# VectorE's order inside the units of a two-branch kernel: three reorderings

## The chip, the cores and the metric

The kernel runs on one core of a Trainium2 chip. The metric is device time in microseconds (us) for one execution. In the profile PE is TensorE, DVE is VectorE, ACT is ScalarE, POOL is GpSimd and SP is SyncE, which here only issues DMAs.

## The reference

The result is `x` plus two branches, in fp32. One is a spectral filter on the layer-normed input, the other a mixture of eight experts of which all eight are chosen, so that the routing only weighs them.

```python
xn = _layernorm(x)                                   # x: (1, 2048, 512)
def _A_ref(x, w_r, w_i):
    X = jnp.fft.rfft2(x, axes=(-2, -1)) * (w_r + 1j * w_i)
    return jnp.fft.irfft2(X, s=(S, D), axes=(-2, -1))
def _B_ref(x, wg, w1, w2):                           # E=8, K=8, D=512, F=1792
    gates = softmax(x @ wg)                          # all 8 kept and normalised
    h = gelu(einsum("nd,edf->nef", x, w1))
    y = einsum("nef,efd->ned", h, w2)
    return einsum("ne,ned->nd", cw, y)
return x + _A_ref(xn, A_w_r, A_w_i) + _B_ref(xn, B_wg, B_w1, B_w2)
```

## The kernel before

**Expert work.** The hidden columns of all experts are cut into 56 chunks of 256. The first two run in a plain stage (`mm1`, `mm2`, with its side work listed in `plan`, L793), which ends at about 138 us. The other 54 run in pairs, each pair on one half of the tokens at a time: 27 pairs by 2 halves are the **units** u = 0 to 53 of the loop at L1301. A product of two 2x2-blocked matrices is done with Strassen's scheme, in Winograd's form: seven block products for the first layer (`layer1`, L991) and seven for the second (`layer2`, L1133), so a unit is 14 products. Each product is 12 matmuls of 128x128 by 128x512, because each fp32 operand is split into a high and a low fp32r part (`high` casts on ACT, `low` subtracts on DVE or POOL) and three of the four partial products are kept. In every product the eight matmuls on the high part of the moving operand come first, and the four on its low part last.

**Steps.** A unit has seven steps n = 0 to 6. `layer1` is a generator with three parts per step; `layer2` of the unit before, called `second`, runs one product a step, woven in between. So TensorE's order in a unit is, with the bank of PSUM each is summed into: a11 (B), b22 (C), a12 (B), T3 (C), s2 (A), b11 (B), s1 (A), b21 (B), s4 (A), T1 (C), s3 (B), T4 (C), a22 (B), T2 (A). Names with a or s first are the first layer's weights, b and T the second layer's hidden blocks. Several products are summed into a bank that still holds the one before: T3 goes on top of b22 in C, b21 on top of b11 in B, T4 on top of T1 in C. DVE adds a bank to the result first (`into`, shown as `acc<-C`, `acc<-B`, `acc<-A`), and the next product on this bank waits for that.

**The start of a unit.** Step 0 multiplies a11 into B, and ACT copies B into bank A (`copy_of(Z, X)`, shown as `COPY A<-B`), where the next sums grow. So ACT needs bank A to be free, that is, DVE's `acc<-A` of the T2 product, the last of the unit before. Product a12 goes on top of B and waits for ACT's copy. After its copy ACT casts the high part of T1, and POOL makes T1's low part. DVE's work around this point is, in the order of the program: `c<-B,c` (B's sum into the fourth block), `c<-c` (`less`, it ends the unit's arithmetic), `hs<-c,hs` (low part of h22, block b22), `acc<-A`, `hs<-c,hs` (low part of T3), the filter step of the slot at n = 0, `acc<-C` (b22's product), `c<-c,cwb` (a block weighted by the gates).

**Filter work.** The Fourier filter is cut into 214 small chunks of DVE and ACT work, some with TensorE work (`filtered`, L426). The loop gives them out in slots: `slot_pe` (L864) takes the next chunk and puts its TensorE part down, `slot_dve` (L873) puts the rest down. Slots stand at n = 0, 2, 3 and 5, and at n = 4 in even units, if the next chunk is of the right kind: a chunk has a cost (1.4 for a step with TensorE work and for `multiply`; 1.3, 1.0 or 0.8 for radix-4, twiddle, `combine` and the like), and the slots at 4 and 5 ask for a chunk without TensorE work under 1.35 (5 also takes one with). Chunks come in this order: a forward transform with TensorE (units 1 to 5), radix and twiddle steps, `multiply` and `combine` in turn, more radix steps (units 6 to 22), an inverse transform with TensorE (22 to 26), and the same for the odd columns (27 to 52, with the steps that are DVE's alone in 32 to 47). A TensorE chunk of the forward transform begins with a fold: `us<-us`, an add or subtract on the tile that the next-but-one matmul will need.

**What sets the order.** From unit 1 on, every instruction of PE, DVE, ACT and POOL is pinned to the order in which the Python code makes it (`strict` and `pin`); DMAs are not. So the order of lines in the loop is the order in each engine's queue. POOL's work is the splitting and summing of weights (`ua`, `us`, `va`, `vs`, `s`, `raw`) and three of the low parts of hidden blocks.

Of the kernel before, what the change touches and what calls it, by code (L numbers as in the profile page):

```python
# [21 lines left out]
NB = S // P  # L22
# [97 lines left out]
def body(ctx: ExitStack, tc: tile.TileContext, io):  # L120
# [168 lines left out]
    def make(m):  # L289
        xn = normed[m] = small("xn", [P, D])  # L290
        nc.vector.tensor_scalar(
            xn, acc[:, TILES[m], :], mv[:, m, 0:1], rstd[:, m : m + 1], op0=ALU.subtract, op1=ALU.mult
        )
        yield 0.5

    def turn(m):
        cast(m, psf.tile([P, D], F32, name="psf"))
        yield 0.8
# [105 lines left out]
    V, A, T = tc.nc.vector, tc.nc.scalar, tc.nc.tensor  # L404
# [17 lines left out]
    def copied():  # L422
        next(copy)
        yield 0.0

    def filtered(p):  # L426

        R = ROW[p]
# [2 lines left out]
        sgn_op = ALU.add if p == 0 else ALU.subtract  # L431
        out, of = [], {}
# [4 lines left out]
        def op(fn, *args, **kw):  # L437
            return pin(fn(*args, **kw))  # L438
# [15 lines left out]
        def table(b):  # L454
            if b % 2 == 0:
                of["D"] = wide("D", F32R)
            t = of["mb", b] = of["D"][:, (b % 2) * 2 * WIDE : (b % 2) * 2 * WIDE + 512].rearrange("p (h c) -> p h c", h=2)
            move(r32(t), mbd[b // 4][b % 4])
# [8 lines left out]
        for k in range(NB + 3):  # L467
            def pe(k=k):
                if 0 <= k - 2 < NB:
                    of["px"] = psf.tile([P, 512], F32, name="psf")[:, :R2]  # L470
                    u = of["u"]
                    products(of["px"], [(u[:, hu, j, :], of["fd"][:, h, j, :R2]) for hu, h in PASSES for j in range(2)])
                if 0 <= k - 3 < NB:
                    mb, X = of.pop(("mb", k - 3)), of.pop(("X", k - 3))
                    of["py"] = psf.tile([P, 512], F32, name="psf")[:, :R2]
                    products(of["py"], [(mb[:, h, c * P : (c + 1) * P], X[:, c, hx]) for c in range(2) for h, hx in PASSES])

            def dve(k=k):
                X = None
                if k < NB:  # L480
                    u1 = of["us", k]
                    op(V.tensor_tensor, u1[:, :2], u1[:, :2], u1[:, 2:], op=sgn_op)
                if 0 <= k - 2 < NB:
                    X = quarters("BC"[k % 2])[:, :, :, :R2].rearrange("p i h (c r) -> p i h c r", c=2)
                    of["X", k - 2] = X
                    px = of["px"].rearrange("p (c r) -> p c r", c=2)
                    op(A.copy, X[:, 0, 0], px)
                    low(X[:, 0], px)
                if k - 3 == 0:
                    of["Y"] = ft.tile([P, NB, 2, P + 1], F32, name="Y")[:, :, :, :RY]  # L490
                if 0 <= k - 3 < NB:
                    op(A.copy, of["Y"][:, k - 3], of["py"].rearrange("p (c r) -> p c r", c=2)[:, :, :RY])
                if 0 <= k - 1 < NB:
                    u1 = of.pop(("us", k - 1))
                    u = of["u"] = ft.tile([P, 2, 2, P], F32R, name="uz")
                    op(A.copy, u[:, 0], u1[:, :2])
                    low(u, u1[:, :2])
                if X is not None:
                    op(A.mul, X[:, 1, :, 0], r32(X[:, 0, :, 1]), -1.0)
                    op(A.copy, X[:, 1, :, 1], r32(X[:, 0, :, 0]))  # L500
                if k + 1 < NB:
                    part(k + 1)
                if 0 <= k - 1 < NB:
                    table(k - 1)

            chunk(dve, 1.4, pe)

# [285 lines left out]
    def plan():  # L793

        s0, s1, sp = sums(0), sums(1), spread()
        g0, g2, g1, g3 = (gates((t,)) for t in TS)

        def one(it):
            return islice(it, 1)

        def raw_wb():
            nonlocal raw
            raw = load(io["wb"][0])
            yield

        def results(bs):
            for b in bs:
                nc.sync.dma_start(res[b], acc[:, b, :])
            yield

        return deque([
            ([make(4)], [stored(0)]),
            ([make(5)], [stored(1), logits_a((0,))]),
            ([make(6)], [logits_b((0,)), turn(4)]),
            ([make(7)], [one(g0), ln_stats(8, 2), turn(5), g0]),
            ([], [turn(6)]),
            ([], [turn(7), ln_stats(10, 1)]),
            ([], [ln_stats(11, 2), logits_a((2,))]),
            ([ln_stats(13, 2)], [logits_b((2,)), ln_stats(15, 1), chain, plain_store("b11", 0)]),
            ([one(g2), make(8)], [g2, one(s0), plain_store("b21", 0)]),  # L820
            ([make(9)], [turn(8), one(s0)]),
            ([make(10), make(11)], [turn(9), one(s0), plain_store("b22", 0)]),
            ([], [turn(10), one(s0)]),
            ([], [turn(11), one(s0)]),
            ([], [logits_a((1,)), one(s0), copied()]),
            ([], [logits_b((1,)), one(s0), copied()]),
            ([one(g1)], [s0]),
            ([make(12)], [g1]),
            ([make(13)], [turn(12)]),
            ([make(14)], [turn(13)]),  # L830
            ([make(15)], [turn(14)]),
            ([], [turn(15), plain_store("b11", 1)]),
            ([one(s1)], [logits_a((3,)), plain_store("b21", 1)]),
            ([], [logits_b((3,)), one(sp), plain_store("b22", 1)]),
            ([one(g3)], [one(sp), g3, one(s1), raw_wb()]),
            ([], [one(sp), results(range(4))]),
            ([one(s1)], [sp, results(range(8, 12))]),
            ([], [one(s1), results(range(4, 8))]),
            ([one(s1)], []),
            ([one(s1)], []),  # L840
            ([], [one(s1)]),
            ([], [s1]),
            ([], []),
        ])
# [25 lines left out]
            todo.append(dve)  # L870
            return not pe

    def slot_dve():  # L873

        while todo:
            todo.pop(0)()

    ahead = {}
    step1, handed = iter(()), 0
# [100 lines left out]
    def less(dst, a, b):  # L980
        pin(nc.vector.tensor_sub(dst, a, b))
# [9 lines left out]
    def layer1(c, i, w, hs, old):  # L991
# [124 lines left out]
        yield  # L1116
        if not last:
            less(h12, h22, h12)
        if not first:
            low(hs, "b22", h22)  # L1120
        yield
        if last:
            weigh(s, s, 1, 0)
            high(hs, "b21", s)
# [8 lines left out]
    def layer2(c, i, w, hs):  # L1133

        fresh = {0, 1, 2, 3} if c == 0 else set()

        def into(slot, z):
            to = acc[:, slot, i]
            if slot in fresh:
                fresh.remove(slot)  # L1140
                copy_of(to, z)
            else:
                plus(to, z, to)

        for b, a, tag, slot in (
            ("b22", "s4", "C", 0), ("T3", "s3", None, 2), ("b11", "a11", "B", 0), ("b21", "a12", None, 1),
            ("T1", "s1", "C", 0), ("T4", "a22", None, 3), ("T2", "s2", "A", 0),
        ):
            if tag:
                z = bank({"b22": "B", "b11": "C"}.get(b, tag) if (c, i) == (0, 0) else tag)  # L1150
            product(z, w[a], hs[b], tag is not None)
            into(slot, z)
            yield

# [146 lines left out]
    for u in range(2 * N2):  # L1301
# [31 lines left out]
        if end:  # L1333
            assert not chunks
            raw2 = raw[:, 2 * F2 : 3 * F2]
            nc.sync.dma_start(raw2, io["wb"][c][:, 2 * F2 : 3 * F2])
            y = ft.tile([P, NB, 2, P + 1], F32R, name="Y").rearrange("p a b c -> p (a b c)")
            both = [
                y[:, k * 4 * D : (k + 1) * 4 * D].rearrange("p (h k d) -> p h k d", h=2, k=2) for k in range(2)
            ]  # L1340
            ident = ft.tile([P, 2, 2, P], F32R, name="uz")
            ident = r32(ident.rearrange("p a b c -> p (a b c)"))[:, :P]
            nc.sync.dma_start(ident, idd)
            for n in "ABCD":
                y = wide(n)
                spots += [y[:, k * D : (k + 1) * D] for k in range(2)]
        for n in range(7):
            next(one)
            if u and not end and (n == 2 or n == 0 and u > 1 or n == 5 and chunks and (chunks[0][0] or chunks[0][2] < 1.35)):
                if slot_pe() and n == 5:  # L1350
                    slot_dve()
            if n == 4 and u % 2 == 0 and 0 < u and not end and chunks and not chunks[0][0] and chunks[0][2] < 1.35:
                slot_pe()
            if i:
# [10 lines left out]
            if n in (2, 3):  # L1365
                slot_dve()
            next(one)
            if not i:
                weights(n)
            if end:  # L1370
# [64 lines left out]
```

## Time and profile before

| | us |
|---|---|
| median of 3 runs | 2308.05 |
| lowest and highest | 2306.32 and 2308.71 |
| the profiled execution | 2307.34 |
| span of its trace | 2305.5 |
| plain stage, up to about | 138 |
| a unit with no TensorE work of the filter (7 to 21, 33 to 47) | 38.2 to 39.2 |
| a unit of the forward transform (2 to 5, 28 to 31) | 43.3 to 45.6 |

The granted TensorE clock is full throughout. A row of the profile's groups reads: source line, engine, operation, tile written and tiles read without buffer numbers, shapes, count. Nearly all instructions of the expert work have one line, L105, where a helper records them; the filter's have L438. A tile read tells where it lies: `A`, `B`, `C`, `psf` and `p` are banks of PSUM where a product is read out of them, while on L438 `A`, `B`, `C`, `D`, `Y`, `us` and `uz` are tiles in SBUF, as are `c`, `hs`, `cwb`, `acc`, `raw` and `s`. In the timeline a row has start, duration, engine, line, operation, names, shapes, count, and in brackets the time that the engine was idle before it and what ended that. A matmul's record is about 0.39 us long though the next starts 0.2275 us later, so a gap in TensorE's work shows as idle time only from 0.16 us on; differences of start times show all of it.

### The profile page before, as it was taken

To read this page: it belongs to the slowest core of one execution; us is meant where nothing else is said; L and a number is where in the kernel's file an instruction comes from. 1 tells how busy PE (TensorE), PEld (TensorE's weight loads), DVE (VectorE), ACT (ScalarE), POOL (GpSimd) and SP (SyncE) were. 2 spreads that over 40 slices of the span, in tenths; PEclk is the share of its full clock that TensorE was granted. 3 is DMA by queue.
4 is the path that set the end of the run, shared out by engine and by line. 5 is a ranking of instruction groups with operands and counts; after the bars stand their busy time and mean duration, and the time that the engine had idled before them with its cause. 6 is when DMAs were issued, how large, how long until landed. Compare 5 with 4: busy or idle time off the path is not lost.

```text
span 2305.5 us, 27801 instructions
## 1 busy us (share of the span) xinstructions
PE 2290.5 (99%) x10478; PEld 1891.8 (82%) x10478; DVE 1872.5 (81%) x1753; ACT 1123.0 (49%) x1559; POOL 1415.1 (61%) x790
## 2 busy tenths in 40 slices
PE   9999999999999999999999999999999999999999
PEld 7778888888888888888888888888888888888887
DVE  8757778798889988877777777898889888876776
ACT  6556554444444445444444554454444445444442
POOL 3355565677567766755555556676666666745563
PEclk9999999999999999999999999999999999999999
DMA  7896776676677667688777776767676666788773
GB/s 254 306 359 244 286 249 246 233 256 237 243 267 258 242 246 265 233 295 293 284 272 247 260 245 230 259 213 246 226 257 226 234 232 240 246 311 282 280 276 133
DMA packets 123717, 588.57 MB, mean 255 GB/s; under 512 B 13600, under 2 KB 16288, under 8 KB 66880
## 3 DMA queue, kind: packets, MB, share of 16 engines
q1 hardware_dynamic: 122784, 574.06, 70.1%
q10 hardware_dynamic: 800, 12.74, 1.4%
q8 instruction: 83, 1.36, 0.2%
q14 instruction: 50, 0.41, 0.0%
HBM read 550.96 MB, written 48.37 MB: 260 GB/s over the span
## 4 chain that ended last, share of the span: by engine, by line
PE 84%; DVE 11%; DMA 1%; ACT 1%; issue 1%; POOL 1%; SPq 0%; ACTq 0%; POOLq 0%; DVEq 0%
PE B L105 33%; PE A L105 22%; PE C L105 22%; DVE c L105 4%; PE psf L438 4%; PE p L105 2%; DVE acc L105 2%; DVE Y L438 2%; DVE hs L105 2%; PE psf L105 1%; DVE B L438 1%; DMA hs<-xs_T 1%; DMA res<-acc 0%; DVE xr L105 0%; ACT A L105 0%
## 5 line engine op out<-in xcount | busy, mean ns | idle before, releaser
L105 POOL TENSOR_TENSOR hs<-c,hs 128x1024 fp32r<-128x1024 f32 x161 | 427.3, 2654 | 347.3 <-ACT hs L105 343.3
L105 ACT CAST hs<-c 128x1024 fp32r<-128x1024 f32 x375 | 394.2, 1052 | 149.7 <-DVE c L105 75.6
L105 PE MATMUL A<-xr,us 128*128 128x512 f32 x1920 | 463.3, 390 | 0.0
L105 PE MATMUL B<-xr,ua 128*128 128x512 f32 x1884 | 456.5, 391 | 3.5 <-DVE c L105 1.8
L105 PE MATMUL C<-hs,vs 128*128 128x512 f32 x1884 | 454.6, 390 | 0.0
L105 PEld LDWEIGHTS A<-xr,us 128*128 128x128 f32 x1920 | 359.7, 188 | 74.6
L105 PEld LDWEIGHTS B<-xr,ua 128*128 128x128 f32 x1884 | 352.6, 188 | 83.3 <-ACT A L105 5.4
L105 PEld LDWEIGHTS C<-hs,vs 128*128 128x128 f32 x1884 | 353.0, 188 | 73.3
L105 DVE TENSOR_TENSOR hs<-c,hs 128x1024 fp32r<-128x1024 f32 x214 | 320.6, 1515 | 6.2 <-ACT hs L105 6.2
L105 DVE TENSOR_TENSOR c<-c 128x1024 f32<-128x1024 f32 x212 | 320.5, 1512 | 0.1
L105 DVE TENSOR_TENSOR acc<-C,acc 128x1024 f32<-128x1024 f32 x207 | 252.1, 1218 | 69.7 <-PE C L105 69.5
L105 PE MATMUL B<-hs,va 128*128 128x512 f32 x1248 | 301.6, 390 | 0.0
L105 PEld LDWEIGHTS B<-hs,va 128*128 128x128 f32 x1248 | 233.4, 188 | 48.8 <-DVE c L105 0.5
L105 DVE TENSOR_TENSOR acc<-B,acc 128x1024 f32<-128x1024 f32 x103 | 125.9, 1223 | 160.2 <-PE B L105 160.0
L105 ACT ACTIVATE c<-c 128x1024 f32<-128x1024 f32 x108 | 114.8, 1063 | 256.6 <-DVE c L105 256.4
L105 ACT COPY c<-A 128x1024 f32<-128x1024 f32 x108 | 109.8, 1017 | 231.5 <-PE A L105 201.0
L105 POOL TENSOR_TENSOR ua<-raw,ua 128x512 fp32r<-128x512 f32 x81 | 133.9, 1653 | 129.5 <-ACT ua L105 129.5
L105 DVE TENSOR_TENSOR c<-c,cwb 128x1024 f32<-128x1024 f32 x108 | 182.5, 1689 | 37.6 <-ACT c L105 37.6
L105 POOL TENSOR_TENSOR va<-raw,va 128x512 fp32r<-128x512 f32 x81 | 142.9, 1764 | 86.1 <-ACT va L105 86.1
L105 PE MATMUL C<-hs,va 128*128 128x512 f32 x660 | 162.3, 395 | 3.1 <-DVE acc L105 2.0
L105 PE MATMUL A<-hs,vs 128*128 128x512 f32 x636 | 153.4, 390 | 0.0
L105 PE MATMUL B<-xr,us 128*128 128x512 f32 x636 | 153.2, 390 | 0.0
(188 smaller groups left out, 2970.2 us busy)
## 6 DMA issues: line engine op xcount, KB each, us to landing
xr<-xs_T SPq DMA_DIRECT2D x212, 1024.0 KB, 6.3
xr<-xs_b SPq DMA_DIRECT2D x161, 1024.0 KB, 5.1
cwb<-cwd SPq DMA_DIRECT2D x124, 256.0 KB, 5.7
raw<-in_wa SPq DMA_DIRECT2D x27, 1024.0 KB, 4.9
raw<-in_wb SPq DMA_DIRECT2D x27, 1024.0 KB, 5.0
xs_T<-Y SPq DMA_DIRECT2D x8, 1024.0 KB, 6.2
us<-xfd SPq DMA_DIRECT2D x32, 256.0 KB, 2.7
D<-mbd SPq DMA_DIRECT2D x32, 256.0 KB, 4.2
```

The lines of the kernel that those rows point to most:

```text
L105: return lambda *args, **kw: self.order(made(*args, **kw))
L438: return pin(fn(*args, **kw))
```

## The change

It does four things, all in the order of instructions; the instructions, their tiles and their sizes stay the same, and TensorE's, POOL's and SP's orders do too.

- **Bank A ahead of h22's low part.** In `layer1`'s step 6 a `yield` moves, so that `low(hs, "b22", h22)` comes in the third part of the step instead of the second. The product T2 of `second` and its `acc<-A` lie between the two.
- **A slot at the end of step 1.** If the next chunk has no TensorE work and costs under 1.35, it is put down at the end of step 1 and not in step 2, where it stood behind `acc<-B` of product b11. This holds in units 6 to 11, 13 to 22 and 32 to 47.
- **Folds last.** A fold is put down behind the rest of its chunk. In units 1 to 4 the chunk of step 5 comes ahead of the weighting of h22, its fold waits until the end of step 6, and in units 2 to 4 the sum `acc<-C` of product T4 waits until after step 6's first part (`hold`).
- In the plain stage `make(13)` is done one place earlier.

```diff
@@ filtered
+    folds = []
...
-            def dve(k=k):
+            def fold(k=k):
+                u1 = of["us", k]
+                op(V.tensor_tensor, u1[:, :2], u1[:, :2], u1[:, 2:], op=sgn_op)
+
+            def dve(k=k, fold=fold):
                 X = None
-                if k < NB:
-                    u1 = of["us", k]
-                    op(V.tensor_tensor, u1[:, :2], u1[:, :2], u1[:, 2:], op=sgn_op)
...
+                if k < NB:
+                    folds.append(fold)
@@ plan
-            ([make(12)], [g1]),
-            ([make(13)], [turn(12)]),
+            ([make(12), make(13)], [g1]),
+            ([], [turn(12)]),
@@
-    def slot_dve():
+    def slot_dve(keep_folds=False):
 
         while todo:
             todo.pop(0)()
+            while folds and not keep_folds:
+                folds.pop()()
@@ layer1
             less(h12, h22, h12)
+        yield
         if not first:
             low(hs, "b22", h22)
-        yield
@@ layer2
+            wait = hold and b == "T4"
...
             product(z, w[a], hs[b], tag is not None)
+            if wait:
+                yield
             into(slot, z)
@@ the loop over units
+        filled = hold = False
         for n in range(7):
             next(one)
-            if u and not end and (n == 2 or n == 0 and u > 1 or n == 5 and chunks and (chunks[0][0] or chunks[0][2] < 1.35)):
+            if hold and n == 6:
+                next(second)
+            if u and not end and (n == 2 and not filled or n == 0 and u > 1 or n == 5 and chunks and (chunks[0][0] or chunks[0][2] < 1.35)):
                 if slot_pe() and n == 5:
                     slot_dve()
+                elif n == 5 and u < 5:
+                    hold = u > 1
+                    slot_dve(True)
...
             next(one)
+            if n == 6 and folds:
+                folds.pop()()
+            filled = n == 1 and u > 1 and not end and chunks and not chunks[0][0] and chunks[0][2] < 1.35
+            if filled:
+                slot_pe()
+                slot_dve()
```

DVE's queue from the end of unit 16 to the middle of unit 17, before; the first row is B's sum in step 6 of unit 16, `acc<-A` is T2's product, the two `hs<-c,hs` the low parts of b22 and of T3, `B<-Y` the filter's step of slot 0, and the last three rows are the drain of b11 from B, the radix step of slot 2 and the low parts of T4 and T2:

```order
L105 TENSOR_TENSOR c<-B,c 128x1024
L105 TENSOR_TENSOR c<-c 128x1024
L105 TENSOR_TENSOR hs<-c,hs 128x1024
L105 TENSOR_TENSOR acc<-A,acc 128x1024
L105 TENSOR_TENSOR hs<-c,hs 128x1024
L438 TENSOR_TENSOR B<-Y 128x8x128
L105 TENSOR_TENSOR acc<-C,acc 128x1024
...
L105 TENSOR_TENSOR c<-c 128x1024
L105 TENSOR_TENSOR acc<-B,acc 128x1024
L438 TENSOR_TENSOR Y<-Y 128x4x2x128
L105 TENSOR_TENSOR hs<-c,hs 128x1024 x2
```

The same stretch of DVE's queue now:

```order
L105 TENSOR_TENSOR c<-B,c 128x1024
L105 TENSOR_TENSOR c<-c 128x1024
L105 TENSOR_TENSOR acc<-A,acc 128x1024
L105 TENSOR_TENSOR hs<-c,hs 128x1024 x2
L440 TENSOR_TENSOR B<-Y 128x8x128
L105 TENSOR_TENSOR acc<-C,acc 128x1024
...
L105 TENSOR_TENSOR c<-c 128x1024
L440 TENSOR_TENSOR Y<-Y 128x4x2x128
L105 TENSOR_TENSOR acc<-B,acc 128x1024
L105 TENSOR_TENSOR hs<-c,hs 128x1024 x2
```

`acc<-A` has moved ahead of b22's low part, which now stands next to T3's low part and the filter step; the radix step has moved ahead of `acc<-B`.

DVE's queue at the end of unit 3, steps 5 and 6, before; the first row is the sum into h22, `us<-us` the fold, `C<-psf,C` and `uz<-us,uz` the rest of the chunk, `acc<-C` T4's product, and the second `c<-B,c` B's sum:

```order
L105 TENSOR_TENSOR c<-B,c 128x1024
L105 TENSOR_TENSOR c<-c,cwb 128x1024
L438 TENSOR_TENSOR us<-us 128x256
L438 TENSOR_TENSOR C<-psf,C 128x260
L438 TENSOR_TENSOR uz<-us,uz 128x256
L105 TENSOR_TENSOR acc<-C,acc 128x1024
L105 TENSOR_TENSOR c<-B,c 128x1024
L105 TENSOR_TENSOR c<-c 128x1024
```

The same stretch now:

```order
L105 TENSOR_TENSOR c<-B,c 128x1024
L440 TENSOR_TENSOR C<-psf,C 128x260
L440 TENSOR_TENSOR uz<-us,uz 128x256
L105 TENSOR_TENSOR c<-c,cwb 128x1024
L105 TENSOR_TENSOR c<-B,c 128x1024
L105 TENSOR_TENSOR acc<-C,acc 128x1024
L105 TENSOR_TENSOR c<-c 128x1024
```

B's sum now stands behind the weighting `c<-c,cwb` and ahead of `acc<-C`, and the fold has left the stretch: it comes behind b22's low part.

## The prediction

> **What bounds the kernel now.** First the page's busy shares and its groups, since they say which engine is full and which instructions have no fixed length.
>
> ```profile
> PE 2290.5 (99%) x10478; PEld 1891.8 (82%) x10478; DVE 1872.5 (81%) x1753; ACT 1123.0 (49%) x1559; POOL 1415.1 (61%) x790
> L105 DVE TENSOR_TENSOR hs<-c,hs 128x1024 fp32r<-128x1024 f32 x214 | 320.6, 1515 | 6.2 <-ACT hs L105 6.2
> L105 DVE TENSOR_TENSOR acc<-C,acc 128x1024 f32<-128x1024 f32 x207 | 252.1, 1218 | 69.7 <-PE C L105 69.5
> L105 DVE TENSOR_TENSOR c<-c,cwb 128x1024 f32<-128x1024 f32 x108 | 182.5, 1689 | 37.6 <-ACT c L105 37.6
> ```
>
> TensorE is busy 99% of 2305.5 us, and this change gives it neither more nor less to do. So only its gaps can change: the change can take gaps away or make new ones. The group rows hold the second clue. The same VectorE shape takes 1.22 us where it reads a bank of PSUM (`acc<-C`) and 1.5 to 1.7 us on average where both inputs lie in SBUF (`hs<-c,hs`, `c<-c,cwb`): something holds the latter up. Next, the waits of TensorE, and of the engines it waits for.
>
> ```profile
> PE C L105 <- DVE acc L105: 2.0, 4, 0.6
> PE B L105 <- DVE c L105: 1.8, 2, 1.3
> PE B L105 <- ACT A L105: 1.7, 8, 0.2
> ACT A L105 <- DVE acc L105: 41.6, 26, 1.9
> ```
>
> The columns are sum, times, longest. The third row is the start of a unit: a12 waits for ACT's copy of B into A, which by the fourth row waits for VectorE's `acc<-A`. The second row is B's sum at the ends of units 1 and 3. The first is T4's wait for T1's product to leave C. A gap costs more than its idle time. Between starts of products, which lie 12 x 0.2275 = 2.73 us apart, each of the third row's gaps costs 0.51, so eight of them 4.1 us; the second row's two gaps cost 1.5 and 0.7 (worked below). All that the change aims at is therefore about 6.4 us, 0.3%.
>
> Then the timeline of one odd unit, 17, with VectorE, ScalarE, TensorE and POOL together; it starts with a11 at 781.68.
>
> ```profile
> 781.13 1.88 DVE L105 TENSOR_TENSOR c<-c 128x1024 f32<-128x1024 f32 x1
> 781.68 2.89 PE L105 MATMUL B<-xr,ua 128*128 128x512 f32 x12
> 781.88 2.27 POOL L105 TENSOR_TENSOR va<-raw,va 128x512 fp32r<-128x512 f32 x1
> 782.92 2.31 DVE L105 TENSOR_TENSOR hs<-c,hs 128x1024 fp32r<-128x1024 f32 x1
> 784.41 2.89 PE L105 MATMUL C<-hs,vs 128*128 128x512 f32 x12
> 784.74 1.66 POOL L105 TENSOR_TENSOR vs<-s,vs 128x512 fp32r<-128x512 f32 x1 [0.58 <-ACT vs L105]
> 785.16 1.21 DVE L105 TENSOR_TENSOR acc<-A,acc 128x1024 f32<-128x1024 f32 x1
> 786.30 1.21 DVE L105 TENSOR_TENSOR hs<-c,hs 128x1024 fp32r<-128x1024 f32 x1
> 786.46 1.00 ACT L105 COPY A<-B 128x1024 f32<-128x1024 f32 x1 [1.80 <-DVE acc L105]
> 787.37 1.05 ACT L105 CAST hs<-c 128x1024 fp32r<-128x1024 f32 x1
> 787.43 1.21 DVE L438 TENSOR_TENSOR B<-Y 128x1024 f32<-128x1024 f32 x1
> 787.51 3.03 PE L105 MATMUL B<-xr,ua 128*128 128x512 f32 x12 [0.22 <-ACT A L105]
> 788.50 2.41 POOL L105 TENSOR_TENSOR hs<-c,hs 128x1024 fp32r<-128x1024 f32 x1 [2.11 <-ACT hs L105]
> 788.56 1.21 DVE L105 TENSOR_TENSOR acc<-C,acc 128x1024 f32<-128x1024 f32 x1
> 789.70 2.29 DVE L105 TENSOR_TENSOR c<-c,cwb 128x1024 f32<-128x1024 f32 x1
> 790.38 2.89 PE L105 MATMUL C<-hs,vs 128*128 128x512 f32 x12
> 795.32 1.31 DVE L105 TENSOR_TENSOR c<-c 128x1024 f32<-128x1024 f32 x1
> 795.49 3.41 POOL L105 TENSOR_TENSOR hs<-c,hs 128x1024 fp32r<-128x1024 f32 x1
> 798.76 1.23 DVE L105 TENSOR_TENSOR acc<-B,acc 128x1024 f32<-128x1024 f32 x1 [2.14 <-PE B L105]
> ```
>
> Read the ends. `c<-c` ends at 783.01; POOL's `va`, recorded from 781.88, ends at 784.15, 1.14 later; `hs<-c,hs` ends at 785.23, 1.08 after that. POOL's `vs` ends at 786.40, 1.17 after 785.23, and the second `hs<-c,hs` ends at 787.51, 1.11 after that. They take strict turns: a VectorE instruction with two inputs in SBUF and a POOL instruction never run at once, and the waiting time is inside the recorded durations. `acc<-A` and `acc<-C`, which read PSUM, keep 1.21 with POOL busy beside them. Over the whole trace, whenever a POOL instruction stood waiting as one such VectorE instruction ended, POOL went next (66 cases of 66), and the VectorE instruction after it ended 1.08 after POOL: 2.39 us on average, against 1.21 without a POOL instruction waiting. The last POOL row shows the price of a low part made there: 795.49 + 3.41 = 798.90, less the end of `c<-c` at 796.63, is 2.27.
>
> **The change part by part. Bank A first.** In unit 17, `acc<-A` now follows `c<-c`, at 782.95 to 784.15, beside POOL's `va`. The low part of b22 loses its wait for `va` in the queue but still ends at 784.15 + 1.08 = 785.23, as today; `vs` still waits for it and ends at 786.40; T3's low part still ends at 786.40 + 1.08 = 787.48. So VectorE gains no time here, and the copy gains: bank A is free at 784.15, a11's product is complete some 0.2 after 784.41, so ACT copies at about 784.66 instead of 786.46. The gap before a12 goes: -0.51.
>
> Now what comes queued behind that copy. ACT's cast of T1 follows 0.91 later (786.46 to 787.37) and POOL's low part of T1 1.13 after that (787.37 to 788.50). Today POOL is ready at 788.50, when the filter step `B<-Y` is already running; it loses to it, then delays only `c<-c,cwb`, which nobody waits for soon. After the change it is ready at 784.66 + 0.91 + 1.13 = 786.70, while T3's low part runs until 787.48. By the turns above POOL goes next, 787.48 + 2.27 = 789.75; `B<-Y` ends at 789.75 + 1.08 = 790.83; `acc<-C`, behind it in VectorE's queue, runs from 790.76 to 791.97. T3 goes on top of C and starts at 792.0, not at 790.38: **+1.6 net**, the saved 0.51 included. Bounds of this unseen meeting: if `B<-Y` keeps its place, -0.51; if it waits in full, +1.6. I take the full wait, because the rows above give it every time.
>
> "The Trainium skill", page "SBUF — State Buffer", section "Who interferes with whom", speaks for the dearer end, against this change: a VectorE tensor_tensor with both inputs in SBUF and a GpSimd instruction reading SBUF share a port under a lock that is held for a whole instruction, and one input from PSUM avoids it. The trace agrees (2.31 for `hs<-c,hs` at 782.92, 1.21 for `acc<-C` at 788.56 beside POOL). By that rule the step costs 2.27 + 1.08; without it, 1.21.
>
> Whether POOL is ready before T3's low part ends is the hinge: unit start + 5.0 against the end of `c<-c` + 4.5. In unit 17 the lead is 787.48 - 786.70 = 0.8. The smallest leads are near 0.3, in units with a `multiply` step, as 13:
>
> ```profile
> 629.58 2.89 PE L105 MATMUL C<-hs,vs 128*128 128x512 f32 x12
> 630.93 1.21 DVE L105 TENSOR_TENSOR hs<-c,hs 128x1024 fp32r<-128x1024 f32 x1
> 632.06 0.68 DVE L438 TENSOR_TENSOR A<-Y,D 128x516 f32<-128x516 f32 x1
> 635.08 2.89 PE L105 MATMUL C<-hs,vs 128*128 128x512 f32 x12
> 643.56 1.30 POOL L105 TENSOR_TENSOR ua<-raw,ua 128x512 fp32r<-128x512 f32 x1
> 644.84 1.48 POOL L105 TENSOR_TENSOR s<-s,raw 128x512 f32<-128x512 f32 x1
> 645.08 1.51 DVE L438 TENSOR_TENSOR Y<-B,A 128x258 f32<-128x258 f32 x1
> ```
>
> Here POOL is ready at 629.58 + 0.2 + 0.91 + 1.13 = 631.82 and T3's low part ends at 632.12 (630.93 + 1.21, less the 0.02 by which ends overlap). POOL goes until 634.39, the two halves of the step end at 634.94 and 635.55, `acc<-C` at 636.69, T3 starts at 636.72: +1.64 on 635.08.
>
> **The filled hole.** In even units VectorE waits 2.7 us for b11, a POOL instruction and a radix step (about 1.2 + 1.1) fit, and b21 waits for TensorE as before: 0. In odd units of the saturated kind the step meets POOL's low part (796.63 to 798.90) and ends at 799.98, so `acc<-B` ends at 801.2, with b21 due at 795.84 + 5.46 = 801.3 today and later with the delay above; the delay also moves VectorE. I put 0.25, bounds 0 and 1.2. In units like 13 the step is two short halves. They meet POOL's `ua` and `s<-s,raw` one after the other (the last row shows a half taking 1.51 so): from 644.85, four turns of 1.2, 0.35, 1.2 and 0.35 end at 647.95, `acc<-B` ends at 649.1, and b21 is due at 636.72 + 4 x 2.73 = 647.64: +1.4, bounds 0 and 1.6.
>
> **Folds and hold.** At the end of unit 3:
>
> ```profile
> 263.19 1.52 DVE L438 TENSOR_TENSOR us<-us 128x256 f32<-128x256 f32 x1
> 264.25 2.89 PE L105 MATMUL A<-hs,vs 128*128 128x512 f32 x12
> 264.98 1.18 DVE L438 TENSOR_TENSOR uz<-us,uz 128x256 fp32r<-128x256 f32 x1
> 266.08 1.21 DVE L105 TENSOR_TENSOR acc<-C,acc 128x1024 f32<-128x1024 f32 x1
> 267.21 1.21 DVE L105 TENSOR_TENSOR c<-B,c 128x1024 f32<-128x1024 f32 x1
> 268.48 0.73 PE L105 MATMUL B<-xr,ua 128*128 128x512 f32 x2 [1.34 <-DVE c L105]
> ```
>
> T2 starts at 264.25, so a11 of unit 4 could start at 266.98; it starts at 268.48, 1.5 late, after B's sum ends at 268.42. Without the fold (1.52) and `acc<-C` (1.13) ahead of it, that sum ends near 266.1 and the gap goes: -1.5. The other gap (0.5 idle in the waits' second row) goes likewise, -0.7. What is late next is the fold itself, but its reader is two matmul steps on, and the DMA that refills `us` has a unit's time. `acc<-C` waits behind B's sum while C's next writer, b22, comes one product later, 2.73 us: covered, and if the cover went it would cost about 1.1 twice. Doing `make(13)` earlier in the plain stage, and the later folds, are hidden by TensorE's 99%: 0.
>
> **The sum.** By the same reading of each unit: five saturated odd units (7, 17, 21, 33, 43) 5 x (1.6 + 0.25) = 9.3; four with `multiply` (13, 15, 39, 41) 4 x (1.64 + 1.4) = 12.2; three saturated with a shorter step (11, 35, 45) 3 x 1.1 = 3.3; two short ones (37, 47) 2 x 1.05 = 2.1; units 9 and 19, where four products of ACT's stand between copy and cast so that POOL isn't early, 2 x 0.6 = 1.2 from the fill; phase one -2.2; T4's waits in odd units, -0.5 as VectorE has slack after the delay. Together +25.4. The profiled execution took 2307.34, so 2332.7; it lies 0.7 below the median of 2308.05. I predict **2333**.
>
> **The rivals.**
>
> *Faster.* The one mechanism is that POOL's low part of T1 does not get in ahead of the filter step: ACT is ready later than I reckon (it has other casts queued near the copy), or VectorE's next instruction wins the turn. Its point of decision is whether POOL is ready before T3's low part has ended, unit start + 5.0 in my sum. For it: the lead is only 0.3 in six units. Against it: it needs 0.8 in the others, and 66 cases of 66. Then the 4.1 and 2.2 stand: 2301.
>
> *Only the saturated units collide.* Those with a lead near 0.3 (13, 15, 37, 39, 41, 47) escape at T3, and with it most of their 14.3; phase one and the rest stay, and some of the fill's cost: about +14, near 2322.
>
> *It cancels.* The new order is refilled by other waits at the same length, for example TensorE's gap of 0.5 before a12 becomes one of 0.5 before T3, which a partial overlap of POOL would give: 2304 to 2312.
>
> **How the numbers follow.** Forecast 0.70, own range 2322 to 2344: 25.4 less or more the bounds of the fill (12.2 to 5.8 without it; 1.2 more in each of five units with it). Only the saturated 0.10, cancelled 0.07, faster 0.13. The range of 8 in 10 takes the first two with their bounds: 2312 to 2346. A measurement of this kernel can tell about 0.2%, 4.6 us, from no change. Faster by more: 0.13; within: 0.07; slower: 0.80.
>
> **What would show it.** In TensorE's waits the row for `ACT A` should be gone and `PE C <- DVE acc` have some 14 more waits, of about 2 us each, at T3 in odd units 7 to 21 and 33 to 47. In POOL's timeline T1's low part should begin at unit start + 5 to 6, ahead of the filter step, which then lasts 3.4. ACT's wait for `acc<-A` (41.6) should fall. `PE B <- DVE acc` should show b21 in units 13, 15, 39 and 41. The gap of 1.34 before unit 4 should be gone. Units 23 to 31 and 48 to 52 should last as long as before. If POOL's low part lies behind the filter step, the forecast is wrong and the faster rival right; if the delays stand at T3 but b21 does not wait, only the fill's price was.

## The result and the profile after

| | before | after |
|---|---|---|
| median, us | 2308.38 (4 runs) | 2338.38 (4 runs) |
| lowest and highest | 2306.32 and 2308.81 | 2336.62 and 2340.45 |
| the profiled execution | 2307.34 | 2338.59 |
| span of its trace | 2305.5 | 2336.8 |

The ratio of after to before is 1.0132, with a 95% interval of 1.0115 to 1.015: the change makes the kernel 30 us slower. The forecast was 2333 in a range of 2312 to 2346.

TensorE's waits come first, as before the change. The columns are sum, times, longest:

```profile
PE C L105 <- DVE acc L105: 26.1, 20, 2.0
PE B L105 <- DVE acc L105: 4.0, 5, 0.8
PE B L105 <- DVE D L105: 0.8, 1, 0.8
```

The rows `ACT A` (1.7) and `DVE c` (1.8) are gone, so the two gaps that the change aimed at are closed. In their place C's row went from 2.0 to 26.1, and a row for b21 (`PE B <- DVE acc`) has appeared. The third row belongs to the last unit and is explained below.

The same stretch of unit 17 as in the prediction; its a11 now starts at 791.23, 9.55 later than before:

```profile
790.68 1.88 DVE L105 TENSOR_TENSOR c<-c 128x1024 f32<-128x1024 f32 x1
791.23 2.89 PE L105 MATMUL B<-xr,ua 128*128 128x512 f32 x12
791.43 2.29 POOL L105 TENSOR_TENSOR va<-raw,va 128x512 fp32r<-128x512 f32 x1
792.48 1.21 DVE L105 TENSOR_TENSOR acc<-A,acc 128x1024 f32<-128x1024 f32 x1
793.61 3.45 DVE L105 TENSOR_TENSOR hs<-c,hs 128x1024 fp32r<-128x1024 f32 x2
794.16 1.00 ACT L105 COPY A<-B 128x1024 f32<-128x1024 f32 x1
794.29 1.69 POOL L105 TENSOR_TENSOR vs<-s,vs 128x512 fp32r<-128x512 f32 x1 [0.57 <-ACT vs L105]
795.07 1.05 ACT L105 CAST hs<-c 128x1024 fp32r<-128x1024 f32 x1
796.20 3.11 POOL L105 TENSOR_TENSOR hs<-c,hs 128x1024 fp32r<-128x1024 f32 x1 [0.22 <-ACT hs L105]
796.69 2.89 PE L105 MATMUL B<-xr,ua 128*128 128x512 f32 x12
796.99 3.41 DVE L440 TENSOR_TENSOR B<-Y 128x1024 f32<-128x1024 f32 x1
800.32 1.21 DVE L105 TENSOR_TENSOR acc<-C,acc 128x1024 f32<-128x1024 f32 x1
801.59 3.02 PE L105 MATMUL C<-hs,vs 128*128 128x512 f32 x12 [2.01 <-DVE acc L105]
```

`acc<-A` runs at once, beside POOL's `va`, and a12 starts 2.73 after b22, without a gap. But POOL's low part of T1 is ready at 796.20, while the second `hs<-c,hs` (T3's low part) still runs to 797.06. POOL goes next and ends at 799.31; the filter step `B<-Y`, recorded from 796.99, lasts 3.41 instead of 1.21; `acc<-C` behind it ends at 801.53, and T3 has waited 2.01. In before's time, 9.55 less, the prediction had 789.75 for POOL's end and 792.0 for T3; the trace gives 789.76 and 792.04.

The busy shares hardly show it: TensorE goes from 99% to 98%, VectorE from 81% to 82%. To see where the time goes, the differences of TensorE's start times are added up for each product, less what its matmuls take undisturbed:

| lost starts, us | before | after |
|---|---|---|
| a11 (units 2 and 4) | 2.4 | 0.1 |
| a12 | 4.1 | 0.0 |
| T3 | 0.0 | 30.0 |
| b21 | 0.0 | 5.6 |
| T4 | 5.7 | 5.6 |
| closing products, behind the last unit's T2 | 0.5 | 1.9 |

Together that is +30.5. The remaining 0.8 stands ahead of unit 2: eight matmuls between 12 and 16 us ran at half pace (see the end), which cost 1.6, and half of it was made up in the plain stage. Such scatter ahead of unit 2 is ordinary: unit 1's last product starts at 176.1 before, at 176.8 after, and between 175.8 and 176.4 in the experiments, with `make(13)` moved or not. The spans differ by 31.3.

### The profile page after: what moved, and what is told of

It reads as the page before. It is cut to its first block, busy times and chain, and to the rows that moved or that the text cites. A ratio compares the mean times of both kernels' runs of the same rounds, so it can differ in the third digit from the quotient of the medians.

```text
span 2336.8 us, 27806 instructions
## 1 busy us (share of the span) xinstructions
PE 2297.0 (98%) x10478; PEld 1894.1 (81%) x10478; DVE 1918.3 (82%) x1753; ACT 1124.2 (48%) x1559; POOL 1398.5 (60%) x790
## 4 chain that ended last, share of the span: by engine, by line
PE 77%; DVE 19%; issue 2%; DMA 1%; ACT 1%; POOL 0%; SPq 0%; ACTq 0%; POOLq 0%; DVEq 0%
PE B L105 29%; PE A L105 21%; PE C L105 19%; DVE c L105 7%; PE psf L440 4%; DVE acc L105 4%; DVE Y L440 3%; PE p L105 3%; DVE hs L105 2%; PE psf L105 1%; DVE B L440 1%; DMA cwb<-cwd 1%; DMA res<-acc 0%; ACT A L105 0%; DVE xr L105 0%
## 5 line engine op out<-in xcount | busy, mean ns | idle before, releaser
L105 DVE TENSOR_TENSOR c<-c 128x1024 f32<-128x1024 f32 x212 | 333.0, 1571 | 0.1
L105 DVE TENSOR_TENSOR hs<-c,hs 128x1024 fp32r<-128x1024 f32 x214 | 313.1, 1499 | 3.7 <-ACT hs L105 3.7
L105 POOL TENSOR_TENSOR ua<-raw,ua 128x512 fp32r<-128x512 f32 x81 | 118.9, 1468 | 161.8 <-ACT ua L105 161.8
L105 DVE TENSOR_TENSOR c<-c,cwb 128x1024 f32<-128x1024 f32 x108 | 172.2, 1594 | 33.0 <-ACT c L105 33.0
L105 POOL TENSOR_TENSOR va<-raw,va 128x512 fp32r<-128x512 f32 x81 | 138.1, 1705 | 77.0 <-ACT va L105 77.0
L105 DVE TENSOR_TENSOR c<-B,c 128x1024 f32<-128x1024 f32 x107 | 130.3, 1218 | 31.0 <-PE B L105 30.7
```

What stands on the lines that cost most here:

```text
L105: return lambda *args, **kw: self.order(made(*args, **kw))
```

## The experiments

The theory was the prediction's: a VectorE instruction with both inputs in SBUF and a POOL instruction take turns; once bank A is drained early, POOL's low part of T1 comes a turn ahead of the filter step, and T3 pays. Each kernel was compared with the kernel before on the same chip (medians 2307.3 to 2308.3).

### 1. Bank A first, alone

The kernel before with this edit only:

```diff
             less(h12, h22, h12)
+        yield
         if not first:
             low(hs, "b22", h22)
-        yield
```

> The kernel before with only the move of h22's low part behind acc<-A. Theory (POOL's low part of T1 is ready before T3's low part ends, so it goes ahead of the filter step and pushes back the drain of b22, for which T3 waits): the T3 waits stand here as in the full change, 28 us of lost starts in odd units 7 to 21 and 33 to 47, the a12 waits (4.1) are gone, and the end of the last unit loses 1.4; together +25 us, near 2334. Rival (the T3 waits need the radix step put into step 1 too): no wait at T3, only the 4.1 saved, near 2304.

Measured: 2336.76, ratio 1.0126 (1.0112 to 1.014). Waits of TensorE in this kernel:

```profile
PE C L105 <- DVE acc L105: 26.1, 20, 2.0
PE B L105 <- DVE c L105: 1.7, 2, 1.3
```

C's row is the one of the full change, to the digit; a12's row is gone, and the gaps of units 2 and 4 are there as before. This edit alone makes T3's loss, and the radix step in step 1 has no part in it. Without its two drops of the clock (see the end) T3 lost about 28.5 in this trace, and in the full change 30.0 with one drop of 1.6. b21 loses nothing here, so the b21 row belongs to the fill, that is, to the radix step put into step 1.

### 2. The radix step in step 1, alone

```diff
-            if u and not end and (n == 2 or n == 0 and u > 1 or ...
+            if u and not end and (n == 2 and not filled or n == 0 and u > 1 or ...
...
+            filled = n == 1 and u > 1 and not end and chunks and not chunks[0][0] and chunks[0][2] < 1.35
+            if filled:
+                slot_pe()
+                slot_dve()
```

> The kernel before with only the radix step at the end of step 1. Theory (two short halves of a step each lose a turn to a POOL instruction, ahead of the drain of b11): b21 waits about 1.07 in units 9, 13, 15, 39 and 41, and T4's waits in odd units (0.5) go; together +5, near 2313; the a12 waits stay. Rival (b21 waits only because T3's delay has set VectorE back): no b21 wait, near 2308.

Measured: 2314.32, ratio 1.0026 (1.0016 to 1.0035). b21 lost 6.2 in all: 1.28 and 1.21 in units 9 and 19, and 0.55 to 0.65 in 13, 15, 35, 39, 41 and 45. So the fill costs time by itself, and the rival falls; but the price sits partly in other units than expected. Without T3's delay VectorE meets POOL at another moment: in unit 13 the two halves lasted 2.63 and 1.52 here, behind a low part of POOL's and `ua`, and 1.53 and 1.52 in the full change, behind `ua` and `s<-s,raw`. The profiled execution, with 2315.72 the slowest of its ten, lost 1.6 more in unit 2, where a fold waited 6.03 for its data, against 3.40 in the trace of before:

```profile
209.44 0.42 DVE L438 TENSOR_TENSOR us<-us 128x256 f32<-128x256 f32 x1 [6.03 <-DMA us<-xfd]
```

Everything behind the fold in VectorE's queue waited too. The third edit, folds last, lets the rest of the chunk go ahead of such a wait; whether it would have saved this loss was not tried.

### 3. Folds last and the held sum, alone

The diff of `filtered`, `layer2` and `hold` as it stands above, without the other edits.

> The kernel before with only the folds last and the sum of T4's product held; the plain stage is that of before. Theory: the gaps at the starts of units 2 and 4 go, 0.7 + 1.6, and nothing else moves: -2.3, near 2306. Rival (the late folds or the held sum make another product wait): within 1 us of before, with a new gap in units 2 to 5.

Measured: 2305.1, ratio 0.9991 (0.9982 to 0.9999). a11 lost nothing any more, no product lost more than before, and the trace is 2.7 shorter. The size is at the edge of what these runs can tell, the gaps' disappearance is not.

### 4. The filter step behind the drain, on top of the full change

```diff
+                alone = slot_pe()
+                late = alone and n == 0 and i == 1
...
-            if n not in (2, 3):
+            if n not in (2, 3) and not late:
                 slot_dve()
             if u != 1 or n:
                 next(second, None)
...
-            if n in (2, 3):
+            if n in (2, 3) or late:
                 slot_dve()
```

> The full change, and in odd units the filter step of slot 0, if it has no TensorE work, stands behind the drain of b22 (acc<-C) instead of ahead of it. Theory (a VectorE instruction with two inputs in SBUF takes turns with POOL, one that reads PSUM does not): acc<-C runs beside POOL's low part of T1, T3 does not wait at all, -28 against the full change, near 2310 or a little under. Rival (POOL holds up whatever VectorE instruction comes next): acc<-C is pushed back by POOL and only the step's own 1.1 is gained, so T3 still waits about 1.1 in each of some 15 units, near 2321.

Measured: 2313.41, ratio 1.0023 (1.0013 to 1.0032). Unit 17 in this kernel:

```profile
783.79 3.45 DVE L105 TENSOR_TENSOR hs<-c,hs 128x1024 fp32r<-128x1024 f32 x2
786.38 3.12 POOL L105 TENSOR_TENSOR hs<-c,hs 128x1024 fp32r<-128x1024 f32 x1 [0.23 <-ACT hs L105]
786.87 2.89 PE L105 MATMUL B<-xr,ua 128*128 128x512 f32 x12
787.16 1.21 DVE L105 TENSOR_TENSOR acc<-C,acc 128x1024 f32<-128x1024 f32 x1
788.29 2.29 DVE L440 TENSOR_TENSOR B<-Y 128x1024 f32<-128x1024 f32 x1
789.60 2.89 PE L105 MATMUL C<-hs,vs 128*128 128x512 f32 x12
```

POOL's instruction stands where it stood and takes as long, but `acc<-C`, which reads PSUM, passes beside it in 1.21, and T3 follows a12 after exactly 2.73. T3's loss fell from 30.0 to 0.5 (all of it in unit 23). So POOL alone does not push a drain back; it does so through an instruction ahead of the drain that has to share with it. The rest was missed: b21 lost 9.9 instead of 5.6, and b11 another 1.0. In unit 17 the filter step now waits its turn later (2.29 at 788.29) and the radix step of step 1 later still (2.32 at 798.49). Without that radix step, in experiment 7, b21 loses nothing.

### 5. POOL's low part in two halves, on top of the full change

```diff
+    def low_halves(hs, n, src):
+        for k in range(2):
+            pin(nc.gpsimd.tensor_tensor(hs[n][:, 1, k], src[:, k], r32(hs[n][:, 0, k]), op=ALU.subtract))
...
-            low(oh, "T1", o11, True)
+            if i:
+                low_halves(oh, "T1", o11)
+            else:
+                low(oh, "T1", o11, True)
```

> The full change; in odd units POOL makes the low part of T1 in two instructions of 128x512 instead of one of 128x1024. Theory (strict turns, one instruction at a time): the filter step gets its turn after the first half, so T3's wait falls by some 1.1 in the units whose step is one long instruction (7, 17, 21, 33, 43 from 2.28 to about 1.15; 11, 35, 45, 37 and 47 likewise) and stays at 1.8 in 13, 15, 39 and 41, whose step is two short ones that each lose a turn: 11 less than the full change, near 2327. Rival (POOL once begun keeps the port until it has nothing left to do): T3's waits stay, 2338.

Measured: 2325.51, ratio 1.0079 (1.0066 to 1.0093). Unit 17:

```profile
791.15 4.22 POOL L105 TENSOR_TENSOR hs<-c,hs 128x512 fp32r<-128x512 f32 x2 [0.23 <-ACT hs L105]
791.93 2.31 DVE L440 TENSOR_TENSOR B<-Y 128x1024 f32<-128x1024 f32 x1
794.16 1.21 DVE L105 TENSOR_TENSOR acc<-C,acc 128x1024 f32<-128x1024 f32 x1
795.43 1.89 PE L105 MATMUL C<-hs,vs 128*128 128x512 f32 x7 [0.90 <-DVE acc L105]
```

`B<-Y` now waits for one half only: 2.31 instead of 3.41, and T3's wait falls from 2.01 to 0.90, by 1.1 as worked out. In 7, 17, 21, 33 and 43 T3 lost 1.17 or 1.18; in 13, 15, 39 and 41, with a step of two short instructions, it stayed at 1.8. So VectorE waits for one instruction of POOL's, not for POOL's whole queue. Units 35 and 45 stayed at 1.8 against the expectation; their step is two `SCALAR_TENSOR_TENSOR` of 128x256, so they belong with 13, which had been overlooked.

### 6. T1's cast later, on top of the full change

```diff
-            high(oh, "T1", o11)
-            low(oh, "T1", o11, True)
+            if i == 0:
+                high(oh, "T1", o11)
+                low(oh, "T1", o11, True)
...
         gelu(X)
+        if old and i:
+            high(oh, "T1", o11)
+            low(oh, "T1", o11, True)
```

> The full change; in odd units ACT's cast of T1, and with it POOL's low part, comes behind the gelu of a12's product, so that POOL isn't ready when T3's low part ends. Theory (the hinge is whether POOL is ready at that moment): the filter step keeps 1.2, T3 does not wait anywhere, about -28, near 2310, with b21's waits (5.6) as in the full change or somewhat longer, since POOL's later instructions shift. Rival (T3 waits because acc<-A stands ahead, whatever POOL does): T3's waits stay, near 2338.

Measured: 2308.51, ratio 1.0006 (0.9997 to 1.0015). Unit 17:

```profile
782.22 3.44 DVE L105 TENSOR_TENSOR hs<-c,hs 128x1024 fp32r<-128x1024 f32 x2
785.59 1.21 DVE L440 TENSOR_TENSOR B<-Y 128x1024 f32<-128x1024 f32 x1
786.73 1.21 DVE L105 TENSOR_TENSOR acc<-C,acc 128x1024 f32<-128x1024 f32 x1
790.27 2.41 POOL L105 TENSOR_TENSOR hs<-c,hs 128x1024 fp32r<-128x1024 f32 x1 [5.68 <-ACT hs L105]
```

VectorE's order is that of the full change, with `B<-Y` ahead of `acc<-C`; only POOL is ready later, and the step keeps its 1.21. T3 lost 0.4 in the whole kernel. This is the hinge of the prediction, moved by hand. That b21's waits vanish as well was not expected; about 5 came back at a22 and 1.2 at the starts of units, where B's sum is late.

### 7. What is left as good

Bank A first with the late slot of experiment 4, folds last and the held sum; no radix step in step 1; the plain stage of before; and in the last unit b22's low part stays ahead of `acc<-A`:

```diff
             less(h12, h22, h12)
+        if last:
+            low(hs, "b22", h22)
         yield
-        if not first:
+        if not first and not last:
             low(hs, "b22", h22)
```

> What the runs so far leave as good: bank A first, folds last and the held sum, the late slot in odd units, no radix step in step 1, the plain stage of before, and in the last unit the low part of b22 where it was before. Theory: a12's gaps (4.1) and the two of units 2 and 4 (2.7) are gone, T3 and b21 don't wait: -6.8 from before, near 2301. Rival (the late step pushes VectorE's later sums back without the fill too): b21 or T4 waits take part of it, 2303 to 2308.

Measured: 2302.19, ratio 0.9979 (0.997 to 0.9988). It beats both kernels. a12, b21 and a11's gaps are empty, T3 loses 0.5, and 1.0 has come back at b11. The closing products lose 0.5 as before and not 1.9.

### 8. A second late slot

```diff
             if n == 4 and u % 2 == 0 and 0 < u and not end and chunks and not chunks[0][0] and chunks[0][2] < 1.35:
-                slot_pe()
+                late = slot_pe()
```

> As e7, and in even units the filter step of the slot at n = 4 stands behind the sum acc<-C of T1's product, for which T4 waits. Theory: acc<-C comes 1.1 sooner there, and the waits at T4 (5.6 in all) are nearly gone: near 2296. Rival (T4's waits come from further back, from B's drains): no change from e7.

Measured: 2309.46, ratio 1.0007 (0.9998 to 1.0016). T4's loss did fall from 5.8 to 0.2, but a22 lost 11.7 where it had lost 0.3, which neither the theory nor its rival had (1.6 of it is a drop of the clock, see the end). Unit 16:

```profile
769.63 1.21 DVE L105 TENSOR_TENSOR acc<-C,acc 128x1024 f32<-128x1024 f32 x1
770.47 1.29 POOL L105 TENSOR_TENSOR vs<-raw,vs 128x512 fp32r<-128x512 f32 x1 [0.74 <-ACT vs L105]
770.76 2.08 DVE L440 TENSOR_TENSOR A<-Y 128x1024 f32<-128x1024 f32 x1
771.72 2.27 POOL L105 TENSOR_TENSOR raw<-raw,s 128x512 f32<-128x512 f32 x1
772.77 2.31 DVE L105 TENSOR_TENSOR c<-c 128x1024 f32<-128x1024 f32 x1
775.00 1.21 DVE L105 TENSOR_TENSOR c<-B,c 128x1024 f32<-128x1024 f32 x1
776.26 4.57 PE L105 MATMUL B<-xr,ua 128*128 128x512 f32 x12 [1.78 <-DVE c L105]
```

In experiment 7 `acc<-C` stood between the filter step and `c<-c`, and POOL ran beside it:

```profile
768.50 1.52 POOL L105 TENSOR_TENSOR vs<-raw,vs 128x512 fp32r<-128x512 f32 x1 [0.73 <-ACT vs L105]
768.78 1.21 DVE L105 TENSOR_TENSOR acc<-C,acc 128x1024 f32<-128x1024 f32 x1
769.92 1.21 DVE L105 TENSOR_TENSOR c<-c 128x1024 f32<-128x1024 f32 x1
```

With the filter step and `c<-c` next to each other each loses a turn, 2.08 and 2.31 for 1.21, and B's sum `c<-B,c`, for which a22 waits, is late. As in the change itself, instructions that have to share came to stand side by side where POOL was ready. b11 lost 1.0 more too, and a11 0.8.

### 9. The second late slot in three units

The line of experiment 8 as `late = slot_pe() and u in (14, 38, 40)`.

> As e7, with the second late slot (the filter step at n = 4 behind acc<-C of T1's product) only in units 14, 38 and 40, where T4 waits 0.85 each and where in e8 no wait of a22 came for it. Theory (elsewhere VectorE would sit idle until T1's product is ready, and the step it used to do in that time then delays B's sum): 2.5 less than e7, near 2299.6. Rival (the waits come back at another product): as e7, 2302.

Measured: 2298.89, ratio 0.996 (0.9946 to 0.9974), the lowest median of all, though its interval overlaps that of experiment 7, which ran on another chip; that something was gained is read from the trace. T4 lost 2.7 instead of 5.8, and a22 0.2. That its waits did not come back at another product is shown. The reason given beside it, that VectorE would otherwise sit idle, is not: experiment 8's rows show lost turns instead.

## Why the prediction held, and where its terms were off

**The bound and the hinge** held. But for 2.4 us of slow clock (1.6 in unit 21, 0.8 ahead of unit 2) only TensorE's gaps changed, and what decided was whether POOL's low part of T1 is ready before T3's low part ends. Experiments 4, 5 and 6 change the instruction behind POOL, POOL's length and POOL's readiness, one each, and T3's wait follows all three.

**T3's terms.** In units 7, 17, 33 and 43 T3 lost 2.27 or 2.28 where a12 had lost 0.47 to 0.49: +1.8 for the term of 1.6. Units 13, 15, 39 and 41 lost 1.8 (1.64), 11, 35 and 45 net 1.3 (1.1), 37 and 47 lost 1.21 (1.05). Each is some 0.2 over. Most of it is the slower start of TensorE after a wait (T3's record in unit 17 lasts 3.02 instead of 2.89), counted in the prediction for the gaps that go and not for those that come.

**Unit 9** is the step that failed. It was taken as safe at T3, since four of ACT's products stand between copy and cast. POOL was late indeed, but the filter step there is two instructions, and POOL came in between them:

```profile
478.74 2.96 DVE L440 SCALAR_TENSOR_TENSOR Y<-Y,C 128x258 f32<-128x258 f32 x2
479.03 2.38 POOL L105 TENSOR_TENSOR hs<-c,hs 128x1024 fp32r<-128x1024 f32 x1 [1.29 <-ACT hs L105]
482.89 1.43 PE L105 MATMUL C<-hs,vs 128*128 128x512 f32 x5 [1.28 <-DVE acc L105]
```

The pair took 2.96 instead of 0.75. T3 lost 1.55 and b21 1.08, net of a12's 0.2 together 2.4, where 0.6 stood. Unit 19 lost 0.1 instead of 0.6.

**The fill.** In 13, 15, 39 and 41 b21 lost 1.06 on average, for 1.4 predicted; the saturated units lost nothing, for 0.25. In unit 13 the two halves did lose a turn each:

```profile
648.30 1.64 POOL L105 TENSOR_TENSOR ua<-raw,ua 128x512 fp32r<-128x512 f32 x1 [0.60 <-ACT ua L105]
648.70 1.53 DVE L440 TENSOR_TENSOR Y<-A,B 128x258 f32<-128x258 f32 x1
649.91 1.48 POOL L105 TENSOR_TENSOR s<-s,raw 128x512 f32<-128x512 f32 x1
650.15 1.52 DVE L440 TENSOR_TENSOR Y<-B,A 128x258 f32<-128x258 f32 x1
651.60 1.21 DVE L105 TENSOR_TENSOR acc<-B,acc 128x1024 f32<-128x1024 f32 x1
652.86 3.02 PE L105 MATMUL B<-hs,va 128*128 128x512 f32 x12 [0.80 <-DVE acc L105]
```

**Phase one** gave 2.3 for 2.2, by experiment 3 and by the trace after:

```profile
264.23 2.89 PE L105 MATMUL A<-hs,vs 128*128 128x512 f32 x12
264.43 1.23 DVE L105 TENSOR_TENSOR c<-B,c 128x1024 f32<-128x1024 f32 x1 [1.97 <-PE B L105]
266.96 2.89 PE L105 MATMUL B<-xr,ua 128*128 128x512 f32 x12
```

B's sum waits for nothing but its product, and unit 4 starts 2.73 after T2. T4's waits in odd units (0.5) went as well; those of even units grew by 0.4.

**Left out of the sum** were three things. In the last unit b22's low part now stands behind `acc<-A`, and is followed by a weighting that meets POOL's closing sums, which wait for the same `acc<-A`:

```profile
2307.18 1.22 DVE L105 TENSOR_TENSOR hs<-c,hs 128x1024 fp32r<-128x1024 f32 x1
2307.35 6.64 POOL L105 TENSOR_TENSOR acc<-acc 128x1024 f32<-128x1024 f32 x2 [10.06 <-DVE acc L105]
2308.32 3.42 DVE L105 TENSOR_TENSOR c<-c,cwb 128x1024 f32<-128x1024 f32 x1
```

The first closing product waited 0.4 longer, for the low part itself. The weighting took 3.42 for 1.22, and a later product waited 1.0 longer, for `D` (the third row of TensorE's waits). Experiment 7 undoes this piece and the loss is gone. Unit 23, whose slot has TensorE work, lost 0.5 at T3. And unit 21 lost 1.6 to the clock, below. With unit 9's 1.8 these make 5.3 of the 5.9 us by which the trace is longer than the sum.

**Luck and the range.** T3's terms were 2.6 too small together, and the fill's, unit 19 included, 3.1 too dear. That they nearly cancel is luck. The stated range does not follow from its terms either: without the fill the four `multiply` units would cost 4 x 1.64 = 6.6 and not 5.8, and the fill's bounds (8.1 less without any of it, 6.8 more with all of it) reach to about 2325 and 2340, not to 2322 and 2344. The measured 2338.38 lies within both.

## What to carry to other kernels

Where two engines take turns, the order within one queue must be read together with the other engine's: an instruction that doesn't share, between two that do, is a place where the other engine runs for nothing. Moving it away can make its neighbours wait: in experiment 8 both did, and experiment 6 shows that they don't if the other engine is not ready then. An early release is worth its gap only if what it sets off does not come in ahead of something that the bound engine needs; here 0.5 was saved at a12 and 2.3 lost at T3. Drains that the bound engine waits for belong ahead of work that can be held up, as experiments 7 and 9 show at both of their places; experiment 8 shows the limit, since there the work that was moved back delayed the next sum.

## What the hardware showed unexpectedly

A wait of 2.0 us was followed once by a slow clock. T3 of unit 21 after the change, and a window on it (length, each engine's busy time, granted clock, DMA share, GB/s):

```profile
957.33 4.61 PE L105 MATMUL C<-hs,vs 128*128 128x512 f32 x12 [2.01 <-DVE acc L105]
957.30:961.30 4.00, 3.98 (x10) 3.12 (x11) 4.00 (x2) 1.04 (x1) 3.93 (x3) 0.57 0.20 54
```

The clock granted was 0.57 over 4 us, and the product took 1.6 more than in unit 17, whose wait was as long (801.59, 3.02). In experiment 1 it happened in units 17 and 21, in experiment 8 once, after a wait of 1.78 in unit 16; the traces of experiments 2 to 7 and 9 have none. So such waits can cost more than their length, in some executions. The Trainium skill, page "TensorE: Matmul & The Clock Gate", section "HAM oscillation — how this bites in real kernels", gives as its rule that idle gaps should not exceed about 3.4 us; here the drops came behind gaps of 1.8 and 2.0, and the measurement decides.

The traces tell the gaps with a drop from those without. By their clock records every drop lasts 3.413, and drops start on a grid of that step: the trace after has another one at 12.07, 277 steps before the one at 957.56, and the two of experiment 1, at 800.19 and 957.20, lie 46 steps apart. Behind the plain stage all the traces together have eleven gaps of 1.78 to 2.01. Four of them lie whole inside one step of the grid, and at the end of each of these steps a drop begins. The other seven are cut by a point of the grid and have none, and gaps of up to 1.57 have none even inside one step. Where the grid lies differs from trace to trace, so the same wait can cost 1.6 more in one execution and not in the next.

The turns themselves have a limit: in the trace after, POOL went first in 80 of 81 meetings in which it was ready before VectorE's instruction ended and VectorE's next was one of 128x1024 with both inputs in SBUF, with leads down to 0.15; the one exception had a lead of 0.07.
